# Clamp of the weight pieces on VectorE, bias tiles loaded one by one, and another order of the attention steps

## The chip, the cores and the metric

The kernel runs on one core of a Trainium2 chip. The metric is the time of one execution on the device in microseconds (us); runs of the same kernel are given by their median. The engines are TensorE (PE in the profile, its weight loads PEld), VectorE (DVE), ScalarE (ACT), GpSimd (POOL) and SyncE (SP), which issues most of the DMA transfers. Each engine works through its own queue in order and waits for others by semaphores.

## What is computed

Attention over 8 batches and 8 heads with a bias that depends on positions, and behind it two matrix products of a gated network on its output:

```python
scores = scale * np.matmul(q, k.transpose(0, 1, 3, 2))        # q, k, v: 8 x 8 x 576 x 64
x = (np.log1p(np.abs(rel)) / psi_i)[..., None]
bias = np.maximum(x @ w1 + b1, 0.0) @ w2                      # 576 x 576 x 8 heads
scores = scores + bias.transpose(2, 0, 1)[None]
attn = np.exp(scores - np.max(scores, axis=-1, keepdims=True))
attn = attn / (np.sum(attn, axis=-1, keepdims=True) + 1e-09)
x = np.matmul(attn, v)                                        # -> 4608 x 512
a, b = x @ moe_w1, x @ moe_w2                                 # 512 x 1024 each
h = a * b @ moe_w3                                            # 1024 x 1024
out = h @ moe_w_out                                           # 1024 x 512
```

The weights of the network arrive as 64-bit floating point and are made into 32-bit numbers on the chip, with integer and floating operations on their two halves.

## The kernel before

**Stages.** A prologue computes the bias for all heads and writes it to the DRAM tile `nb_d`. Then attention runs over 32 units, one for each pair of heads `p` (four) and batch `b` (eight), `u = 8p + b`. Then `w_out` is folded into `w3` (`fold`, 16 steps, and `evict_w`), while the first two weight matrices are made ready in 16 pieces (`split_w`). Last come nine chunks of 512 tokens, eight `up` and `down` steps each, which is dense work for PE.

**A unit of attention.** Its 576 rows for two heads are nine tiles, named 0 to 7 and M (even numbers are the first head, odd the second, M the last 64 rows of both). The steps are named by a letter and a tile:

- `ldk`, `ldq`, `ldv` load (SP); `gk`, `gq` (`op_g`, POOL) split k and q into a rounded part and a rest, `kh`, `kl`, `qh`, `ql`, in two buffers each.
- `S` (`op_S`, PE, L266): scores of a tile into one of two PSUM buffers, in three products.
- `T` (`op_T`, DVE, L277): adds the bias tile `nb`, scales, and finds the maximum. It frees the S buffer; its result is one of four buffers `ts`.
- `E` (`op_E`, ACT, L300): exponential and sum of the row.
- `F` (`op_F`, PE, L321 to L333): transposes. F0 to F3 take the two heads of a row block, FL the last 64 columns of all, FN what is left of M. `H` (`op_H`, L344 on DVE, L346 on ACT) copies each from PSUM to SBUF.
- `W0`, `W1` (`op_W`, PE, L386): product with v for columns 0 to 255 and 256 to 575. `X` (`op_X`) copies it out, `xd` stores it.
- In the last unit of a pair `r`, `R`, `HR`, `rd` make and store the reciprocal sums.
- `c0` to `c7` (in units 1 to 6 of each pair) make one 128 x 512 piece of `w_out` or `w3` into 32 bits by the eight steps of `narrow`: fetch (SP), size (ACT, L128), rest and clamp (POOL, L131 and L134), shift, head and power (DVE, L137, L143, L148), and total, two products on POOL (L151, L152). The raw piece `wi` has one buffer here, and two in the later 16 pieces.

Transposes and W share the PSUM pool `ps_t`, two buffers, taken in the order of PE: six F and one for both W0 and W1 in a unit. A step that takes a buffer waits for the copy that frees the one taken two before.

**What sets the order.** The table `ORDER` gives each step of a unit a time, and unit u is put `u * PERIOD` later; the times only sort the steps, engine by engine, for PE, DVE, ACT and POOL. So steps of up to four units stand interleaved in a queue. The loads' order on SP is chosen by the compiler. The later stages are sorted in the same way by `AT_F`, `PACE_F` (fold), `AT_W1`, `PACE_W` (weight pieces), `AT_X`, `PACE_X` (split of the first chunk's x).

**Bias tiles.** `load_bias` fetches the tiles of a pair in five groups, `02`, `13`, `46`, `57` and `M`, with one buffer each. A group of the next pair is loaded in the last unit of a pair, once both T's that read it are issued.

Of the kernel before, what the change touches and what calls it, by code (L numbers as in the profile page):

```python
# [9 lines left out]
F32 = mybir.dt.float32  # L10
F32R = mybir.dt.float32r
I32 = mybir.dt.int32
U32 = mybir.dt.uint32
AF = mybir.ActivationFunctionType
# [4 lines left out]
P = 128  # L19
# [6 lines left out]
AT_F, PACE_F = 2.50, 3.20  # L26
AT_FOLD = -2.0, -1.4, -1.3, -0.6, 0.0
AT_W1, PACE_W, AT_X, PACE_X = 4.00, 5.70, 37.00, 2.10
# [3 lines left out]
PERIOD = 13.21  # L32
ORDER = {
    "PE": {
        "S6": 0.00, "SM": 0.40, "S5": 1.75, "S7": 5.79, "S4": 6.19, "S3": 7.68, "S2": 9.48, "S1": 9.88, "S0": 15.85,
        "FN": 20.32, "F3": 20.46, "F1": 21.58, "FL": 22.43, "F2": 23.78, "F0": 28.20, "W0": 37.99, "W1": 43.25,
    },
    "DVE": {
        "T6": 0.60, "TM": 1.46, "T5": 4.84, "T7": 6.79, "T4": 7.94, "T3": 8.80, "T2": 10.96, "T1": 11.82, "c4": 16.12,
        "c5": 16.70, "c6": 17.40, "T0": 17.48, "HN": 21.15, "HL": 23.20, "H2": 26.18, "X": 46.49,  # L40
    },
    "ACT": {
        "E6": 2.03, "EM": 4.18, "E5": 5.73, "E7": 10.07, "E4": 11.05, "c1": 12.33, "E2": 12.59, "E3": 13.57,
        "E1": 14.55, "E0": 20.21, "H3": 21.23, "H1": 22.40, "H0": 30.01,
    },
    "POOL": {
        "gq": -7.23, "gk": -2.81, "c3": 13.11, "c2": 13.65, "c7": 17.80,
    },
    "SP": {"ldk": -13.62, "ldq": -15.83, "ldv": 7.34},
}  # L50
AT_R = 23.41
# [14 lines left out]
def relpos_attention_moe(  # L66
# [43 lines left out]
    def narrow(pool, src, n, x, queue, pieces=1):  # L110
# [19 lines left out]
        def rest():  # L130
            nc.gpsimd.tensor_scalar(x, d["lo"].bitcast(U32), 2.0 ** -52, 1.0, op0=ALU.mult, op1=ALU.mult)  # L131

        def clamp():
            nc.gpsimd.tensor_scalar(d["mag"], d["mag"], LEAST, MOST, op0=ALU.max, op1=ALU.min)  # L134
# [54 lines left out]
    nbp = att_r.enter_context(tc.tile_pool(name="nbp", bufs=1, side="right"))  # L189
# [16 lines left out]
    GROUPS = ("02", "13", "46", "57", "M")  # L206
    GROUP = {t: g for g in GROUPS for t in g}

    def load_bias(p, ts):
        if ts == "M":  # L210
            nb = nbp.tile([P, S], F32, name="nbM")
            nc.sync.dma_start(nb[lo], nb_v[2 * p, 512:576, :])
            nc.sync.dma_start(nb[hi, S - 512:S], nb_v[2 * p + 1, 512:576, 0:512])
            nc.sync.dma_start(nb[hi, 0:S - 512], nb_v[2 * p + 1, 512:576, 512:S])
            NB[p, ts] = nb
            return
        nb = nbp.tile([P, 2, S], F32, name=f"nb{ts[0]}")
        h, r0 = int(ts[0]) % 2, int(ts[0]) // 2 * P
        rows = nb_v[2 * p + h, r0:r0 + 2 * P, :].rearrange("(k p) j -> p k j", p=P)
        if h == 0:  # L220
            nc.sync.dma_start(nb, rows)
        else:
            nc.sync.dma_start(nb[:, :, S - 512:S], rows[:, :, 0:512])
            nc.sync.dma_start(nb[:, :, 0:S - 512], rows[:, :, 512:S])
        for k, t in enumerate(ts):
            NB[p, t] = nb[:, k]
# [44 lines left out]
    def op_T(u, t):  # L271

        d = st[u]
        p, b = units[u]
        ts = sm.tile([P, S], F32, name="ts", bufs=NTS)
        mx = sm.tile([P, 1], F32, name="mx", bufs=NTS)
        nc.vector.tensor_tensor_reduce(  # L277
            out=halves(ts), in0=d.pop(("s", t))[:, :, :HS], in1=halves(NB[p, t]),
            op0=ALU.add, op1=ALU.min, scale=-1.0 / SQ, scalar=3.0e38, accum_out=mx,
        )  # L280
        d["t", t] = (ts, mx)
        done = d.setdefault("done", set())
        done.add(t)
        if b == B - 1 and p + 1 < NPAIR and done.issuperset(GROUP[t]):
            load_bias(p + 1, GROUP[t])

# [54 lines left out]
    def move(on, *moves):  # L341
        for o, x in moves:
            if on == "DVE":
                nc.vector.tensor_copy(o, x)  # L344
            else:
                nc.scalar.activation(o, x, AF.Copy)  # L346
# [19 lines left out]
    def op_W(u, n):  # L366
# [4 lines left out]
        if "acc" not in d:  # L371
            d["acc"] = ps_t.tile([P, 2, 512], F32, name="pst")
        acc = d["acc"][:, int(n), 0:qs.stop - qs.start]
# [17 lines left out]
    def op_X(u, n, on):  # L391
        d = st[u]
        d["x"] = sm.tile([P, S], F32, name="x")
        move(on, *((d["x"][:, qs], d["acc"][:, m, 0:qs.stop - qs.start]) for m, qs in enumerate(QS)))
# [6 lines left out]
    def piece_of(i):  # L401
        if i < NF:
            return narrow(cva, moe_w_out[i * P:(i + 1) * P, :], DO, wos[i], nc.sync)
        hf, t = divmod(i - NF, NF)
        return narrow(cva, moe_w3[t * P:(t + 1) * P, hf * 512:(hf + 1) * 512], 512, w3s[t][hf], nc.sync)
# [25 lines left out]
    with ExitStack() as pro:  # L431
# [92 lines left out]
        for G in range(NGRP):  # L524
            at = -LEAD + G * PACE_B
            put(plan, bias_group(G), *(at + d for d in AT_BIAS))
            for ts in GROUPS:
                if G == (NGRP - 1 if ts == "M" else 8 * (int(ts[-1]) // 2) + 7):
                    plan.append((at + AT_BIAS[-1] + LAG_B, len(plan), lambda ts=ts: load_bias(0, ts)))
# [280 lines left out]
```

## Time and profile before

| | |
|---|---|
| three runs | 1258.41, 1259.74, 1261.9 us |
| median | 1259.74 us |
| profiled execution | 1257.73 us, span 1255.9 us, mean granted clock 0.971 |
| PE busy | 1132.2 us (90%) |
| DVE, ACT, POOL busy | 638.9, 521.4, 452.1 us |

The page divides the span into 40 equal slices of 31.4 us; each digit is the busy share of a slice in tenths, and PEclk is the granted clock of TensorE:

```profile
PE   8668878887888788889788999999999999999998
PEld 3246656665666666666466788888888888888887
DVE  8648766776677667767787522222212221313111
ACT  7557756676677667763232221212121212121211
POOL 0347754775477547747677400000000000000000
PEclk9879999999999999999988999999999999999999
```

The first two slices are the prologue, slices 3 to 17 attention, 18 to 22 the fold with the weight pieces, and the rest the `up` and `down` steps. A row of the trace's timeline reads: start, duration, engine, line, operation, output <- inputs, shapes, count, and in brackets how long the engine had been idle and what ended that. In the groups of instructions the bar is followed by total busy time, mean ns of one, and the idle time of the engine just ahead of them with what ended it.

### The profile page before, as it was taken

To read this page: it belongs to the slowest core of one execution; us is meant where nothing else is said; L and a number is where in the kernel's file an instruction comes from. 1 tells how busy PE (TensorE), PEld (TensorE's weight loads), DVE (VectorE), ACT (ScalarE), POOL (GpSimd) and SP (SyncE) were. 2 spreads that over 40 slices of the span, in tenths; PEclk is the share of its full clock that TensorE was granted. 3 is DMA by queue.
4 is the path that set the end of the run, shared out by engine and by line. 5 is a ranking of instruction groups with operands and counts; after the bars stand their busy time and mean duration, and the time that the engine had idled before them with its cause. 6 is when DMAs were issued, how large, how long until landed. Compare 5 with 4: busy or idle time off the path is not lost.

```text
span 1255.9 us, 22540 instructions
## 1 busy us (share of the span) xinstructions
PE 1132.2 (90%) x9092; PEld 881.3 (70%) x9092; DVE 638.9 (51%) x1288; ACT 521.4 (42%) x1039; POOL 452.1 (36%) x342
## 2 busy tenths in 40 slices
PE   8668878887888788889788999999999999999998
PEld 3246656665666666666466788888888888888887
DVE  8648766776677667767787522222212221313111
ACT  7557756676677667763232221212121212121211
POOL 0347754775477547747677400000000000000000
PEclk9879999999999999999988999999999999999999
DMA  7743453446344634431433111111111120200001
GB/s 220 246 151 115 139 198 122 135 136 201 122 136 136 201 121 136 135 101 45 137 125 100 51 67 34 57 45 51 51 51 51 36 65 34 68 34 1 23 12 33
DMA packets 61127, 123.13 MB, mean 98 GB/s; under 512 B 9312, under 2 KB 18912, under 8 KB 61024
## 3 DMA queue, kind: packets, MB, share of 16 engines
q1 hardware_dynamic: 59728, 120.21, 29.8%
q10 hardware_dynamic: 1296, 1.49, 0.4%
q8 instruction: 71, 1.16, 0.4%
q14 instruction: 32, 0.26, 0.1%
HBM read 91.76 MB, written 29.92 MB: 97 GB/s over the span
## 4 chain that ended last, share of the span: by engine, by line
PE 72%; DVE 7%; POOL 6%; DMA 6%; ACT 4%; issue 3%; SPq 1%; ACTq 0%; DVEq 0%; POOLq 0%
PE up L652 29%; PE o L677 15%; PE pst L386 12%; PE s L266 8%; PE pst L321 5%; DVE ts L277 4%; ACT pt L346 3%; DMA wi<-in_moe_w_dram 3%; PE bacc L504 2%; POOL wmag L134 2%; DVE x L344 2%; DMA nb_d<-bev 1%; DMA nb<-nb_d 1%; PE pst L332 1%; POOL w L151 1%
## 5 line engine op out<-in xcount | busy, mean ns | idle before, releaser
L277 DVE CUSTOM_DVE_ANT_0 ts<-s,nb 128x576 f32<-128x576 f32 x256 | 188.4, 753 | 131.5 <-PE s L266 95.9
L652 PE MATMUL up<-xh,wh 128*128 128x512 f32 x576 | 225.4, 391 | 0.0
L652 PE MATMUL up<-xh,wl 128*128 128x512 f32 x576 | 225.4, 391 | 0.0
L652 PE MATMUL up<-xl,wh 128*128 128x512 f32 x576 | 225.3, 391 | 0.0
L300 ACT ACTIVATE pp<-ts,mx 128x576 f32<-128x576 f32 x256 | 196.1, 769 | 69.4 <-DVE mx L277 69.4
L660 DVE TENSOR_TENSOR g<-up,a 128x512 f32<-128x512 f32 x72 | 49.7, 690 | 336.0 <-PE up L652 335.9
L677 PE MATMUL o<-w3s,gh 128*128 128x512 f32 x576 | 180.6, 395 | 3.7 <-ACT gh L663 3.7
L638 POOL TENSOR_SCALAR xh<-xr 128x512 fp32r<-128x512 f32 x36 | 23.8, 662 | 437.8 <-DVE xr L634 436.3
L386 PE MATMUL pst<-pt,rv 128*64 128x256 f32 (+1 forms) x1280 | 171.0, 413 | 0.5 <-DVE rt L344 0.5
L266 PE MATMUL s<-kh,qh 64*128 64x288 f32 x640 | 118.7, 363 | 34.5 <-DVE mx L277 31.9
L657 ACT COPY a<-up 128x512 f32<-128x512 f32 x72 | 42.1, 585 | 251.0 <-PE up L652 251.0
L321 PE MATMUL pst<-ident,pp 64*128 64x64 f32 x2304 | 108.3, 226 | 40.7 <-DVE x L344 39.8
L346 ACT ACTIVATE pt<-pst 128x1024 f32<-128x1024 f32 x96 | 96.2, 1025 | 95.1 <-PE pst L321 95.1
L321 PEld LDWEIGHTS pst<-ident,pp 64*128 64x128 f32 x2304 | 100.2, 141 | 47.9 <-issue 44.9
L386 PEld LDWEIGHTS pst<-pt,rv 128*64 128x64 f32 x1280 | 89.1, 139 | 63.3 <-issue 9.7
L677 PEld LDWEIGHTS o<-w3s,gh 128*128 128x128 f32 x576 | 109.5, 191 | 28.3 <-ACT gh L663 5.4
L652 PEld LDWEIGHTS up<-xh,wh 128*128 128x128 f32 x576 | 108.4, 188 | 23.4
L652 PEld LDWEIGHTS up<-xh,wl 128*128 128x128 f32 x576 | 108.4, 188 | 23.3
L652 PEld LDWEIGHTS up<-xl,wh 128*128 128x128 f32 x576 | 108.3, 188 | 23.4
L677 PE MATMUL o<-w3s,gl 128*128 128x512 f32 x288 | 114.5, 398 | 3.6 <-DVE gl L666 3.6
L663 ACT ACTIVATE gh<-g 128x512 fp32r<-128x512 f32 x72 | 45.5, 632 | 171.3 <-DVE g L660 171.3
L266 PEld LDWEIGHTS s<-kh,qh 64*128 64x128 f32 x640 | 64.6, 194 | 58.9 <-DVE mx L277 41.6
(86 smaller groups left out, 1794.6 us busy)
## 6 DMA issues: line engine op xcount, KB each, us to landing
rq<-in_q_dram SPq DMA_DIRECT2D x31, 640.0 KB
wi<-in_moe_w_dram SPq DMA_DIRECT2D x32, 512.0 KB
nb_d<-bev SPq DMA_DIRECT2D x36, 295.5 KB
rv<-in_v_dram SPq DMA_DIRECT2D x32, 320.0 KB
x_d<-x SPq DMA_DIRECT2D x32, 288.0 KB
xr<-x_d SPq DMA_DIRECT2D x36, 256.0 KB
rb<-r_d SPq DMA_DIRECT2D x72, 128.0 KB
rk<-in_k_dram SPq DMA_DIRECT2D x31, 288.0 KB
```

The costliest lines, as they stand in the source:

```text
L134: nc.gpsimd.tensor_scalar(d["mag"], d["mag"], LEAST, MOST, op0=ALU.max, op1=ALU.min)
L266: nc.tensor.matmul(s[:, hf, :HS], Q[x][rows, q0:q0 + P], K[y][rows, h * HS:(h + 1) * HS], start=(m == 0), stop=(m == len(ops) - 1),)
L277: nc.vector.tensor_tensor_reduce(out=halves(ts), in0=d.pop(("s", t))[:, :, :HS], in1=halves(NB[p, t]), op0=ALU.add, op1=ALU.min, scale=-1. ...
L300: nc.scalar.activation(pp, ts, AF.Exp, bias=mx, scale=-1.0, accum_out=sums[p][:, 9 * b + col:9 * b + col + 1])
L321: nc.tensor.transpose(ps[0:n, hf, c0:c0 + 64], x[rows], ident[rows, rows])
L346: nc.scalar.activation(o, x, AF.Copy)
L386: nc.tensor.matmul(o, x[:, c0:c0 + D], m, start=(c == 0), stop=(c == 4 and n_m == len(ms) - 1),)
L652: nc.tensor.matmul(acc, l[:, cc], r, start=(n == 0), stop=(n == 3 * NC - 1))
L657: nc.scalar.copy(a, ps[0])
L660: nc.vector.tensor_tensor(g, ps[1], a, op=ALU.mult)
L663: nc.scalar.activation(gh, g, AF.Copy)
L677: nc.tensor.matmul(d["o", t], l[:, sl], folded[ft][r], start=(ft == 0 and n == 0), stop=(ft == NF - 1 and n == 2),)
```

## The change

- **Clamp**: `clamp` of `narrow` is issued on VectorE, for all 40 pieces.
- **Rest**: for the 24 pieces made during attention `rest` stays on GpSimd; for the 16 later ones it is an activation on ScalarE.
- **Bias tiles**: nine tiles a pair, each loaded by itself into one of eleven buffers, in the order of their T's (`TURNS`). In the last unit but one of a pair the first two tiles of the next pair are loaded; in the last unit the T of each tile is followed by the load of the tile two further on. For the first pair each tile is loaded when its group of bias rows has been written.
- **W and X**: W0 and W1 take a PSUM buffer each, and X is two steps, X0 and X1.
- **Order**: new times for all steps, with a period of 12.49. E, F and H are distributed anew: H1, H0, HL and H2 on ACT, H3, HN, X0 and X1 on DVE; c3 (the clamp) on DVE.
- **Constants**: `AT_F`, `PACE_F` and `AT_X` are smaller.

```diff
@@ -23,32 +23,32 @@
 FIRST = {"ldk": -15.0, "ldq": -14.0, "ldv": -4.0, "gk": -9.0, "gq": -5.0}
 AT_BIAS = -0.7, 1.0, 2.5
 
-AT_F, PACE_F = 2.50, 3.20
+AT_F, PACE_F = 2.00, 2.80
 AT_FOLD = -2.0, -1.4, -1.3, -0.6, 0.0
-AT_W1, PACE_W, AT_X, PACE_X = 4.00, 5.70, 37.00, 2.10
+AT_W1, PACE_W, AT_X, PACE_X = 4.00, 5.70, 28.00, 2.10
 AT_W = 3.5, 0.0, 0.5, 1.2, 2.6, 3.8, 5.5, 7.1, 10.0, 10.6
 
 
-PERIOD = 13.21
+PERIOD = 12.49
 ORDER = {
     "PE": {
-        "S6": 0.00, "SM": 0.40, "S5": 1.75, "S7": 5.79, "S4": 6.19, "S3": 7.68, "S2": 9.48, "S1": 9.88, "S0": 15.85,
-        "FN": 20.32, "F3": 20.46, "F1": 21.58, "FL": 22.43, "F2": 23.78, "F0": 28.20, "W0": 37.99, "W1": 43.25,
+        "S0": 0.00, "S3": 0.41, "S1": 1.76, "S7": 2.29, "S5": 4.20, "S2": 7.21, "SM": 7.62, "S6": 9.04, "F1": 13.82,
+        "F0": 15.23, "S4": 15.85, "FL": 21.04, "F2": 25.88, "F3": 28.79, "W0": 29.67, "FN": 32.16, "W1": 34.51,
     },
     "DVE": {
-        "T6": 0.60, "TM": 1.46, "T5": 4.84, "T7": 6.79, "T4": 7.94, "T3": 8.80, "T2": 10.96, "T1": 11.82, "c4": 16.12,
-        "c5": 16.70, "c6": 17.40, "T0": 17.48, "HN": 21.15, "HL": 23.20, "H2": 26.18, "X": 46.49,
+        "T0": 0.71, "T3": 1.40, "T1": 2.43, "T7": 3.12, "T5": 6.30, "T2": 7.88, "c3": 9.03, "c4": 9.54, "TM": 10.13,
+        "T6": 10.82, "c5": 11.51, "c6": 12.36, "T4": 18.14, "H3": 29.51, "X0": 32.41, "HN": 33.63, "X1": 37.84,
     },
     "ACT": {
-        "E6": 2.03, "EM": 4.18, "E5": 5.73, "E7": 10.07, "E4": 11.05, "c1": 12.33, "E2": 12.59, "E3": 13.57,
-        "E1": 14.55, "E0": 20.21, "H3": 21.23, "H1": 22.40, "H0": 30.01,
+        "E0": 4.39, "E3": 5.18, "E1": 5.97, "c1": 7.61, "E5": 8.21, "E7": 9.29, "E2": 11.03, "E6": 11.82, "EM": 12.61,
+        "H1": 15.02, "H0": 15.97, "E4": 19.29, "HL": 22.61, "H2": 26.60,
     },
     "POOL": {
-        "gq": -7.23, "gk": -2.81, "c3": 13.11, "c2": 13.65, "c7": 17.80,
+        "gk": -8.54, "gq": -6.29, "c2": 10.54, "c7": 12.84,
     },
-    "SP": {"ldk": -13.62, "ldq": -15.83, "ldv": 7.34},
+    "SP": {"ldk": -18.63, "ldq": -14.18, "ldv": 0.74},
 }
-AT_R = 23.41
+AT_R = 22.64
 TILES = "01234567M"
 NPP, NTS, NPS = 7, 4, 2
 
@@ -107,7 +107,7 @@
     LEAST = struct.unpack("<f", struct.pack("<I", 0x38000000))[0]
     MOST = struct.unpack("<f", struct.pack("<I", 0x47EFFFFF))[0]
 
-    def narrow(pool, src, n, x, queue, pieces=1):
+    def narrow(pool, src, n, x, queue, pieces=1, low=nc.scalar):
 
         d = {}
 
@@ -128,10 +128,13 @@
             nc.scalar.activation(d["mag"], f(d["hi"]), AF.Abs)
 
         def rest():
-            nc.gpsimd.tensor_scalar(x, d["lo"].bitcast(U32), 2.0 ** -52, 1.0, op0=ALU.mult, op1=ALU.mult)
+            if low is nc.scalar:
+                nc.scalar.activation(x, d["lo"].bitcast(U32), AF.Copy, scale=2.0 ** -52)
+            else:
+                low.tensor_scalar(x, d["lo"].bitcast(U32), 2.0 ** -52, 1.0, op0=ALU.mult, op1=ALU.mult)
 
         def clamp():
-            nc.gpsimd.tensor_scalar(d["mag"], d["mag"], LEAST, MOST, op0=ALU.max, op1=ALU.min)
+            nc.vector.tensor_scalar(d["mag"], d["mag"], LEAST, MOST, op0=ALU.max, op1=ALU.min)
 
         def shift():
             nc.vector.tensor_scalar(
@@ -186,7 +189,7 @@
     att, att_r = ctx.enter_context(ExitStack()), ctx.enter_context(ExitStack())
     raw = att_r.enter_context(tc.tile_pool(name="raw", bufs=1, side="right"))
     qk = att_r.enter_context(tc.tile_pool(name="qk", bufs=1, side="right"))
-    nbp = att_r.enter_context(tc.tile_pool(name="nbp", bufs=1, side="right"))
+    nbp = att_r.enter_context(tc.tile_pool(name="nbp", bufs=11, side="right"))
     cva = att_r.enter_context(tc.tile_pool(name="cva", bufs=1, side="right"))
     ps_s = att_r.enter_context(tc.tile_pool(name="ps_s", bufs=2, space=PSUM, side="right"))
     vp = att.enter_context(tc.tile_pool(name="vp", bufs=2))
@@ -203,27 +206,24 @@
         return x.rearrange("p (a j) -> p a j", a=2)
 
 
-    GROUPS = ("02", "13", "46", "57", "M")
-    GROUP = {t: g for g in GROUPS for t in g}
-
-    def load_bias(p, ts):
-        if ts == "M":
-            nb = nbp.tile([P, S], F32, name="nbM")
-            nc.sync.dma_start(nb[lo], nb_v[2 * p, 512:576, :])
-            nc.sync.dma_start(nb[hi, S - 512:S], nb_v[2 * p + 1, 512:576, 0:512])
-            nc.sync.dma_start(nb[hi, 0:S - 512], nb_v[2 * p + 1, 512:576, 512:S])
-            NB[p, ts] = nb
-            return
-        nb = nbp.tile([P, 2, S], F32, name=f"nb{ts[0]}")
-        h, r0 = int(ts[0]) % 2, int(ts[0]) // 2 * P
-        rows = nb_v[2 * p + h, r0:r0 + 2 * P, :].rearrange("(k p) j -> p k j", p=P)
-        if h == 0:
-            nc.sync.dma_start(nb, rows)
-        else:
-            nc.sync.dma_start(nb[:, :, S - 512:S], rows[:, :, 0:512])
-            nc.sync.dma_start(nb[:, :, 0:S - 512], rows[:, :, 512:S])
-        for k, t in enumerate(ts):
-            NB[p, t] = nb[:, k]
+    TURNS = sorted(TILES, key=lambda t: ORDER["DVE"]["T" + t])
+
+    def load_bias(p, t, first=False):
+        nb = NB[p, t] if first else nbp.tile([P, S], F32, name="nb")
+        NB[p, t] = nb
+        heads = (0, 1) if t == "M" else (int(t) % 2,)
+        for h in heads:
+            o = nb[(lo, hi)[h]] if t == "M" else nb
+            r0 = 512 if t == "M" else int(t) // 2 * P
+            rows = nb_v[2 * p + h, r0:r0 + o.shape[0], :]
+            if h == 0:
+                nc.sync.dma_start(o, rows)
+            else:
+                nc.sync.dma_start(o[:, S - 512:S], rows[:, 0:512])
+                nc.sync.dma_start(o[:, 0:S - 512], rows[:, 512:S])
+
+    for t in TURNS:
+        NB[0, t] = nbp.tile([P, S], F32, name="nb")
 
     def load(u, which):
         p, b = units[u]
@@ -279,10 +279,12 @@
             op0=ALU.add, op1=ALU.min, scale=-1.0 / SQ, scalar=3.0e38, accum_out=mx,
         )
         d["t", t] = (ts, mx)
-        done = d.setdefault("done", set())
-        done.add(t)
-        if b == B - 1 and p + 1 < NPAIR and done.issuperset(GROUP[t]):
-            load_bias(p + 1, GROUP[t])
+        k = TURNS.index(t)
+        if p + 1 < NPAIR:
+            if b == B - 2 and k < 2:
+                load_bias(p + 1, t)
+            elif b == B - 1 and k + 2 < len(TURNS):
+                load_bias(p + 1, TURNS[k + 2])
 
     def op_E(u, t):
         d = st[u]
@@ -368,9 +370,7 @@
         d = st[u]
         qs, x = QS[int(n)], d["rv"]
         PT, PX = PTX[u % 2]
-        if "acc" not in d:
-            d["acc"] = ps_t.tile([P, 2, 512], F32, name="pst")
-        acc = d["acc"][:, int(n), 0:qs.stop - qs.start]
+        acc = ps_t.tile([P, 2, 512], F32, name="pst")[:, 0, 0:qs.stop - qs.start]
         for c in range(5):
             for h, rows in enumerate((lo, hi)):
                 c0 = (4 * h + c if c < 4 else 8 + h) * D
@@ -390,8 +390,9 @@
 
     def op_X(u, n, on):
         d = st[u]
-        d["x"] = sm.tile([P, S], F32, name="x")
-        move(on, *((d["x"][:, qs], d["acc"][:, m, 0:qs.stop - qs.start]) for m, qs in enumerate(QS)))
+        if "x" not in d:
+            d["x"] = sm.tile([P, S], F32, name="x")
+        move(on, (d["x"][:, QS[int(n)]], d["acc" + n]))
 
     def op_x(u, n):
         p, b = units[u]
@@ -400,9 +401,9 @@
 
     def piece_of(i):
         if i < NF:
-            return narrow(cva, moe_w_out[i * P:(i + 1) * P, :], DO, wos[i], nc.sync)
+            return narrow(cva, moe_w_out[i * P:(i + 1) * P, :], DO, wos[i], nc.sync, low=nc.gpsimd)
         hf, t = divmod(i - NF, NF)
-        return narrow(cva, moe_w3[t * P:(t + 1) * P, hf * 512:(hf + 1) * 512], 512, w3s[t][hf], nc.sync)
+        return narrow(cva, moe_w3[t * P:(t + 1) * P, hf * 512:(hf + 1) * 512], 512, w3s[t][hf], nc.sync, low=nc.gpsimd)
 
     pieces = dict(zip([u for u in range(NU) if 0 < u % B < B - 1], (piece_of(i) for i in range(3 * NF))))
     assert len(pieces) == 3 * NF
@@ -524,9 +525,9 @@
         for G in range(NGRP):
             at = -LEAD + G * PACE_B
             put(plan, bias_group(G), *(at + d for d in AT_BIAS))
-            for ts in GROUPS:
-                if G == (NGRP - 1 if ts == "M" else 8 * (int(ts[-1]) // 2) + 7):
-                    plan.append((at + AT_BIAS[-1] + LAG_B, len(plan), lambda ts=ts: load_bias(0, ts)))
+            for t in TILES:
+                if G == (NGRP - 1 if t == "M" else 8 * (int(t) // 2) + 7):
+                    plan.append((at + AT_BIAS[-1] + LAG_B, len(plan), lambda t=t: load_bias(0, t, True)))
         drive(plan)
 
 
```

## The prediction

> **What bounds the kernel now.** I read busy time by stage first, then one unit of attention instruction by instruction, then the step from one pair of heads to the next, then the chain of waits after attention.
>
> ```profile
> 105.28:542.46 437.18, 375.22 (x5215) 289.85 (x5213) 314.12 (x748) 294.89 (x613) 289.28 (x202) 0.97 0.46 147
> ...
> 567.61:715.30 147.69, 123.70 (x545) 91.40 (x544) 109.14 (x123) 42.82 (x74) 104.35 (x78) 0.92 0.31 97
> 715.30:1255.90 540.60, 536.32 (x2352) 441.60 (x2351) 127.88 (x190) 96.80 (x166) 17.31 (x28) 1.00 0.13 41
> ```
> The columns are length, then busy time of PE, PEld, DVE, ACT, POOL, then granted clock, DMA share, GB/s. The last stage (the second part of the network, 540.6 us) is PE at 99%: the change does not touch it. What can move lies ahead: units 3 to 31 of attention start between 105.28 and 542.46 (28 intervals, PE idle 62 us), and the fold stage, where the weight pieces are made (PE idle 24 us, clock 0.92).
>
> Inside a unit, VectorE and TensorE:
> ```profile
> 253.51 0.34 PE L386 MATMUL pst<-px,rv 128*64 128x64 f32 x4
> ...
> 256.23 0.72 PE L321 MATMUL pst<-ident,pp 64*128 64x64 f32 x16 [1.34 <-DVE x L344]
> ```
> ```profile
> 254.59 0.76 DVE L277 CUSTOM_DVE_ANT_0 ts<-s,nb 128x576 f32<-128x576 f32 x1 [1.57 <-PE s L266]
> ...
> 255.27 0.82 DVE L344 COPY x<-pst 128x256 f32<-128x256 f32 x2
> ...
> 269.99 0.82 DVE L344 COPY x<-pst 128x256 f32<-128x256 f32 x2
> ```
> A unit takes 269.99 - 255.27 = 14.72 us. W1 has ended at 253.85, but its eviction X stands behind a T that waits for an S issued after W1; DVE idles 1.57 us, X starts at 255.27, and PE waits 1.34 us for the PSUM buffer. Two such units together, groups with idle time:
> ```profile
> L266 PE MATMUL s<-kh,qh 64*128 64x288 f32 x40 | 7.2, 350 | 0.4 <-DVE mx L277 0.4
> L321 PE MATMUL pst<-ident,pp 64*128 64x64 f32 x144 | 6.7, 223 | 2.7 <-DVE x L344 2.7
> L332 PE MATMUL pst<-ident,ppM 64*128 64x64 f32 x8 | 1.3, 235 | 0.3 <-ACT pt L346 0.3
> ```
> PE idles 3.4 us in two units, so its own work is 14.72 - 1.7 = 13.0 us a unit.
>
> Between pairs of heads:
> ```profile
> 172.33 0.82 DVE L344 COPY x<-pst 128x256 f32<-128x256 f32 x2
> ...
> 178.02 0.38 SPq L221 DMA_DIRECT2D nb<-nb_d  x1
> ...
> 185.09 0.76 DVE L277 CUSTOM_DVE_ANT_0 ts<-s,nb 128x576 f32<-128x576 f32 x1 [5.50 <-DMA nb<-nb_d]
> ...
> 194.12 0.82 DVE L344 COPY x<-pst 128x256 f32<-128x256 f32 x2
> ```
> The tile of two bias blocks is loaded only after the last T that reads it, 7 us ahead of its next use; that unit takes 21.79 us, 7.07 more than 14.72. There are three such places. Check: 28 x 14.72 + 3 x 7.07 = 433.4 of the 437.2 us.
>
> After attention, one cycle of a weight piece in the chain of waits:
> ```profile
> 643.09 0.79 POOL w L131
> ...
> 643.95 1.97 POOL wmag L134
> 645.92 1.27 POOL w L151
> ...
> 647.22 3.61 DMA wi<-in_moe_w_dram
> ...
> 650.91 0.70 ACT wmag L128
> ...
> 654.96 3.64 DMA wi<-in_moe_w_dram
> ```
> ```profile
> 567.61 0.65 POOL L131 TENSOR_SCALAR w<-wi 128x512 f32<-128x512 uint32 x1
> ...
> 700.03 0.64 POOL L131 TENSOR_SCALAR w<-wi 128x512 f32<-128x512 uint32 x1 [1.79 <-DMA wi<-in_moe_w_dram]
> ```
> Load, rest, clamp, then the previous piece's product frees the buffer for the next load: 654.96 - 647.22 = 7.74 us each, all on POOL and DMA. The 16 pieces take 132.4 us for 15 intervals, 8.8 each with the fold among them.
>
> **The change, part by part.**
>
> (1) The order. Folded into one period, the new list has PE run S0 S3 F2 F1 S1 S7 F0 S4 F3 S5 W0 FN S2 SM FL S6 W1, where F2, F3, W0, FN, W1 belong to two units back and F1, F0, S4, FL to one back. I walk it with the waits of these rows:
> ```profile
> 262.41 0.40 PE L266 MATMUL s<-kh,qh 64*128 64x288 f32 x2
> ...
> 264.04 0.40 PE L266 MATMUL s<-kh,qh 64*128 64x288 f32 x2 [0.18 <-DVE mx L277]
> ```
> ```profile
> 263.22 0.76 DVE L277 CUSTOM_DVE_ANT_0 ts<-s,nb 128x576 f32<-128x576 f32 x1 [0.69 <-PE s L266]
> ...
> 264.02 0.76 DVE L277 CUSTOM_DVE_ANT_0 ts<-s,nbM 128x576 f32<-128x576 f32 x1
> 264.70 0.42 DVE L137 TENSOR_SCALAR wmag<-wmag 128x512 int32<-128x512 int32 x1
> 265.16 0.69 DVE L143 SCALAR_TENSOR_TENSOR wmag<-wi,wmag 128x512 int32<-128x512 int32 x1
> 265.96 0.43 DVE L148 TENSOR_SCALAR wi<-wmag 128x512 int32<-128x512 int32 x1
> ```
> ```profile
> L300 ACT ACTIVATE pp<-ts,mx 128x576 f32<-128x576 f32 x256 | 196.1, 769 | 69.4 <-DVE mx L277 69.4
> ```
> T may start 0.81 after its S (262.41 to 263.22), occupies DVE 0.68 (264.02 to 264.70), and frees the S buffer 0.82 after its start (264.04); an eviction frees its PSUM buffer 0.14 after its end (X above: 256.09 to 256.23). With S at 0.4 to 0.5 start to start, F at 0.5, W0 at 2.3 and W1 at 2.9 (rounded from that same unit), PE goes, from S0 = 0: S3 0.5, F2 0.9, F1 1.4, S1 1.9, S7 2.35, F0 2.8, S4 3.5 (held 0.2 for T1, which waits for S1), F3 4.0, S5 4.5, W0 5.0, FN 7.3, S2 7.5, SM 8.0, FL 8.8, S6 9.3, W1 9.85, next S0 12.75. That is PE's own work again, as the 13.0 above says. Of its releases: X1 now stands ahead of T0 and needs no later S, so it runs as W1 ends (0.2 to 0.8) and F1 at 1.4 finds it done; F0 follows H2 (done 2.7), W0 follows H0 (4.6), FL follows X0 (8.1). W0 and W1 have a PSUM allocation each, eight a period on two buffers where seven stood, and each finds the eviction two back finished. So the 1.34 goes and nothing of its size takes its place; late next would be F0 behind H2, by 0.1 or so. I take **12.9** for a unit without a weight piece.
>
> (2) The clamp in attention. DVE gains one instruction a piece (c3), which I price at 0.42 like L137 above, its nearest row in shape and engine (the other end is POOL's own, 1.97 in the chain of waits). Where it is put is dearer. c3 follows HN, 5.5 to 6 us after S4, and POOL, which starts the next unit's split when S4 frees the k buffer, is then in ql, after kh, kl and qh (the rows show them in the old order):
> ```profile
> 254.36 1.26 POOL L249 TENSOR_SCALAR qh<-rq 128x1280 fp32r<-128x1280 f32 x1
> 255.70 2.92 POOL L250 TENSOR_TENSOR ql<-rq,qh 128x1280 fp32r<-128x1280 f32 x1
> ...
> 259.34 1.42 POOL L250 TENSOR_TENSOR kl<-rk,kh 128x576 fp32r<-128x576 f32 x1
> ```
> ```profile
> 661.45 1.29 POOL L151 TENSOR_TENSOR w<-w,wi 128x512 f32<-128x512 f32 x1
> ```
> ```profile
> 661.51 1.51 DVE L137 TENSOR_SCALAR wmag<-wmag 128x512 int32<-128x512 int32 x1 [1.81 <-POOL wmag L134]
> ```
> The same L137 takes 0.42 beside an idle POOL and 1.51 beside a POOL tensor_tensor, ending 0.28 after it (663.02 against 662.74). So c3 cannot end before ql. The whole split takes 260.76 - 254.36 = 6.40. The chain: S4 + 0.75 (its four steps of PE and the hand-over), split 6.40, +0.28 = S4 + 7.4; c4 0.45 to 0.9, TM and T6 1.36, c5 0.8 (265.16 to 265.96), c6 0.43 give X1 at S4 + 10.4 to 10.9; from X1 over T0, S1, T1 to the next S4 it is 0.40 + 3 x 0.82 = 2.86. Together 13.2 to 13.7; I take **13.5**. [...]
> What is late is X1 again, behind c3 to c6, and F1 behind it. 22 of the 28 units carry a piece: (22 x 13.5 + 6 x 12.9) / 28 = 13.37, a gain of 28 x 1.35 = **38 us**. [...]
>
> (3) Bias tiles singly, eleven buffers. Two tiles of the next pair load a unit early, each other one two T's after its predecessor, so more than 13 us ahead of use against 7 before. Six more DMA issues a pair cost SP about 0.4 each, which nothing waits for. The whole 7.07 should go; I take **20 us** of 21 for three (bounds 0, 21).
>
> (4) The start.
> ```profile
> 69.37 0.76 DVE L277 CUSTOM_DVE_ANT_0 ts<-s,nb 128x576 f32<-128x576 f32 x1 [18.88 <-DMA nb<-nb_d]
> ...
> 74.67 0.76 DVE L277 CUSTOM_DVE_ANT_0 ts<-s,nbM 128x576 f32<-128x576 f32 x1 [4.53 <-DMA nbM<-nb_d]
> ```
> T6 and TM lead unit 0 now, and both wait for late bias; the other seven T's come behind them. In the new order six T's stand ahead of TM, three of them on the early blocks: by 75 us seven are done instead of two. Five T's by 0.8 to 1.2 us (S, T and the S buffer take turns, 0.81 + 0.82 over two buffers) are 4 to 6; with the next unit's first S's close behind I take **6 us** (bounds 0, and 9 for all seven).
>
> (5) The last 16 pieces. Rest goes to ACT (busy 42.8 of 147.7, so 0.65 hides beside the clamp's wait), the clamp to DVE: POOL loses 0.79 + 1.97 a piece. A buffer's chain is then load 3.64, abs 0.70, clamp 0.42, shift 0.42, head 0.69, power 0.43, product 1.29, with six hand-overs some 8.5 us over two buffers, 4.3 a piece; but DVE's instructions with SBUF operands (those four, and wl like head: 2.65) and POOL's two products (2.6) take turns, and three differences of g and x, like head too, come to each second piece (1.0): 6.3, with hand-overs **6.7** where 7.74 stood. In the fold half 0.79 + 1.97 - 0.42 = 2.3 a piece could go, but its steps, the load of x and POOL's differences of the fold also wait: half of it. 8 x 1.0 + 8 x 1.2 is about **17 us** (bounds 0 and 34: PE's idle 24 plus the 8% of clock on 124). AT_F, PACE_F and AT_X only reorder inside this stage.
>
> Sum: 38 + 20 + 6 + 17 = 81. The profiled execution took 1257.73 (span 1255.9); 1257.7 - 81 = 1176.7. The median shown, 1259.74, is 2 us above it: **1179 us**.
>
> **Rivals.**
> [...]
> B, the gains outside the unit fail: the tail stays at POOL's and DMA's pace because loads, x and the fold wait in turn, or the bias loads still collide: 17 to 30 us worse, 1196 to 1209. That is the clamp not doing what it says, too.
> C, the slower side: the piece's load comes late.
> ```profile
> SPq L237 <- POOL ql L250: 119.8, 27, 12.6
> ```
> ```profile
> 253.06 0.33 SPq L123 DMA_DIRECT2D wi<-in_moe_w_dram  x1
> ```
> SP serves loads in a fixed row and idles 119.8 us in the queue ahead of q loads that wait for ql. c1 on ACT now stands ahead of E5, E7 and the rest, 4 us after S4 (T4 behind H3 2.4, E4 0.8 later and 0.8 long). The piece's one buffer comes free with the product behind c6, about 1.4 before the next S4, and the load lands some 3.8 later: a slack of 1.6. If wi comes behind the q load instead, it lands 11 us after S4: ACT and then PE lose about 6 us in 22 units, 132 us: 1179 + 132 = 1311. It decides from 1.6 + 81/22 = 5.3 us of lateness. Against it: wi is issued now at 253.06, just as its buffer comes free.
>
> **How the numbers follow.** The forecast itself has 0.52 (1167 to 1192), A 0.15, B 0.20, something smaller lost in several places 0.07 (1210 to 1250), C 0.06. The range, 1150 to 1218, leaves out C, most of the 0.07 and the far ends of A and B. Changes under 0.3%, 4 us, cannot be told from none: faster 0.92, same 0.02, slower 0.06.
>
> **What would show it.** X spaced 13.3 to 13.7 with pieces and about 12.9 without; no PE idle put down to DVE x of 1.34; c3 as a max/min on DVE of over 1 us ending 0.3 after ql; no wait of T for nb over 2 us between pairs; TM of unit 0 near 74 with six T's ahead; pieces 6.5 to 8 apart, and the last up stage again 540 us long. Long ACT idle ahead of L128 would show C, and would make me wrong.

## The result, and the profile after

The changed kernel takes 1173.92 us (median of four runs, 1170.18 to 1179.22) against 1259.08 us for the kernel before (1253.79 to 1261.9): a ratio of 0.9331, with a 95% interval of 0.9281 to 0.9382. The forecast was 1179. The profiled execution took 1171.91 us with a span of 1170.1, 85.8 less than the 1257.73 of before.

The 40 slices of the page, of 29.3 us each now:

```profile
PE   7669998998999999999999999999999999999998
DVE  8748878888888788849985322213131322213111
POOL 0446665775567467525453000000000000000000
PEclk9889999999999999999999999999999999999999
```

From slice 4 on PE no longer falls to 7, and the dense part begins at slice 22 of shorter slices.

By stage, in the same columns as before (length, busy time of PE, PEld, DVE, ACT, POOL, then granted clock, DMA share, GB/s). The stages are: up to the first S of unit 3, up to that of unit 31, most of unit 31, the fold, and the last part. The last part begins here with the same up step as before; that step starts at 629.14, where it started at 715.13.

```profile
0.00:103.80 103.80, 74.70 (x708) 41.04 (x710) 73.50 (x191) 70.35 (x157) 34.72 (x30) 0.90 0.67 206
103.80:488.65 384.85, 366.69 (x5213) 286.06 (x5213) 328.82 (x742) 313.69 (x639) 248.63 (x178) 1.00 0.53 164
488.65:515.00 26.35, 24.41 (x318) 17.72 (x317) 14.51 (x35) 21.47 (x41) 6.74 (x5) 1.00 0.23 76
515.00:629.14 114.14, 109.30 (x510) 83.87 (x507) 101.17 (x138) 48.39 (x84) 57.42 (x44) 0.99 0.40 126
629.14:1170.10 540.96, 536.82 (x2353) 441.39 (x2351) 129.16 (x192) 97.95 (x168) 18.98 (x30) 1.00 0.13 41
```

The 28 units went from 437.18 to 384.85 us (52.3 less), the start from 105.28 to 103.80 (1.5 less), and everything behind the start of unit 31 from 1255.9 - 542.46 = 713.4 to 681.4 (32 less). The last part is as long as it was (541 us), so these 32 us lie ahead of it: the fold takes 114.1 us instead of 147.5. PE is busy 96% of that time at a clock of 0.99, where it was 84% at 0.92.

One unit with a weight piece in the changed kernel, VectorE and GpSimd together (timeline):

```profile
261.70 0.42 DVE L346 COPY x<-pst 128x256 f32<-128x256 f32 x1 [0.19 <-PE pst L386]
261.85 2.95 POOL L250 TENSOR_TENSOR ql<-rq,qh 128x1280 fp32r<-128x1280 f32 x1
262.47 0.76 DVE L277 CUSTOM_DVE_ANT_0 ts<-s,nb 128x576 f32<-128x576 f32 x1 [0.34 <-PE s L266]
...
263.64 1.45 DVE L137 TENSOR_SCALAR wmag<-wmag 128x512 f32<-128x512 f32 x1
...
268.47 0.48 DVE L346 COPY x<-pst 128x320 f32<-128x320 f32 x1
...
275.27 0.42 DVE L346 COPY x<-pst 128x256 f32<-128x256 f32 x1 [0.19 <-PE pst L386]
...
287.90 0.42 DVE L346 COPY x<-pst 128x256 f32<-128x256 f32 x1 [0.19 <-PE pst L386]
```

X0 comes every 275.27 - 261.70 = 13.57 us with a piece and 287.90 - 275.27 = 12.63 without. c3 (L137 is the clamp here) starts while ql runs and takes 1.45; ql ends at 264.80, c3 at 265.09. The T in front of it, whose operand comes from PSUM, keeps its 0.76 beside the same ql.

Behind a pair of heads, the same view with PE:

```profile
288.06 2.93 POOL L250 TENSOR_TENSOR ql<-rq,qh 128x1280 fp32r<-128x1280 f32 x1
...
288.24 2.80 DVE L307 TENSOR_SCALAR sum<-sum 128x72 f32<-128x72 f32 x1
...
292.36 0.40 PE L266 MATMUL s<-kh,qh 64*128 64x288 f32 x2 [2.55 <-DVE mx L277]
...
292.95 2.86 PE L386 MATMUL pst<-pt,rv 128*64 128x320 f32 x20
```

```profile
303.55 0.42 DVE L346 COPY x<-pst 128x256 f32<-128x256 f32 x1 [0.18 <-PE pst L386]
```

T no longer waits for bias tiles there. But the unit takes 303.55 - 287.90 = 15.65 us: r, a tiny instruction (72 columns), takes 2.80 us beside ql, T's stand behind it, and PE idles 2.55.

### The profile page after: what moved, and what is told of

Its sections match the earlier page's. It is cut to its first block, busy times and chain, and to the rows that moved or that the text cites. A ratio compares the mean times of both kernels' runs of the same rounds, so it can differ in the third digit from the quotient of the medians.

```text
span 1170.1 us, 22602 instructions
## 1 busy us (share of the span) xinstructions
PE 1111.9 (95%) x9092; PEld 870.1 (74%) x9092; DVE 647.2 (55%) x1296; ACT 551.9 (47%) x1087; POOL 366.5 (31%) x286
## 4 chain that ended last, share of the span: by engine, by line
PE 51%; DVE 5%; ACT 3%; DMA 3%; POOL 1%; issue 1%; ACTq 0%; SPq 0%; DVEq 0%; POOLq 0%
PE up L653 30%; PE o L678 15%; DMA wi<-in_moe_w_dram 3%; PE pst L386 2%; PE s L266 2%; DVE wmag L137 1%; DVE ts L277 1%; PE pst L323 1%; POOL w L154 1%; PE wacc L611 1%; ACT pp L302 1%; DVE w3l L604 1%; ACT wmag L128 0%; DVE wmag L140 0%; ACT ppM L302 0%
## 5 line engine op out<-in xcount | busy, mean ns | idle before, releaser
L277 DVE CUSTOM_DVE_ANT_0 ts<-s,nb 128x576 f32<-128x576 f32 x288 | 207.5, 753 | 41.8 <-PE s L266 27.2
L678 PE MATMUL o<-w3s,gh 128*128 128x512 f32 x576 | 177.8, 390 | 0.3 <-ACT gh L664 0.3
L348 ACT ACTIVATE pt<-pst 128x1024 f32<-128x1024 f32 x128 | 126.3, 1013 | 34.5 <-PE pst L323 34.5
L386 PEld LDWEIGHTS pst<-pt,rv 128*64 128x64 f32 x1280 | 88.1, 137 | 62.4 <-issue 11.5
L323 PE MATMUL pst<-ident,pp 64*128 64x64 f32 x2304 | 104.9, 224 | 11.1 <-ACT ppM L302 10.7
L266 PE MATMUL s<-kh,ql 64*128 64x288 f32 x640 | 96.6, 295 | 2.4 <-POOL ql L250 2.4
```

Of the source, the lines that this page charges most:

```text
L266: nc.tensor.matmul(s[:, hf, :HS], Q[x][rows, q0:q0 + P], K[y][rows, h * HS:(h + 1) * HS], start=(m == 0), stop=(m == len(ops) - 1),)
L277: nc.vector.tensor_tensor_reduce(out=halves(ts), in0=d.pop(("s", t))[:, :, :HS], in1=halves(NB[p, t]), op0=ALU.add, op1=ALU.min, scale=-1. ...
L323: nc.tensor.transpose(ps[0:n, hf, c0:c0 + 64], x[rows], ident[rows, rows])
L386: nc.tensor.matmul(o, x[:, c0:c0 + D], m, start=(c == 0), stop=(c == 4 and n_m == len(ms) - 1),)
L678: nc.tensor.matmul(d["o", t], l[:, sl], folded[ft][r], start=(ft == 0 and n == 0), stop=(ft == NF - 1 and n == 2),)
```

## The experiments

All times are medians; each edit is made on the changed kernel (1173.92 us) unless said otherwise. X0 spacings are read as above.

### The clamp later on VectorE

```diff
-"c3": 9.03, "c4": 9.54, "TM": 10.13,
+"c3": 11.40, "c4": 11.45, "TM": 10.13,
```

> The changed kernel with c3 and c4 put behind T6 on VectorE, so that TM and T6 no longer stand behind a clamp that waits for ql. If the clamp's wait beside ql is what makes units with a weight piece longer than those without (13.58 against 12.63 us in the trace), these units fall to 12.6 to 12.9: 22 units by 0.7 to 0.9, some 15 to 20 us off 1174, about 1156. If they are longer only because VectorE has four more instructions a piece, the period stays at 13.4 to 13.6 and the time within 4 us of 1174. If X1, which follows c6, comes later for it, units grow and the time is above 1180.

Measured: 1153.18 us (1150.34 to 1154.71), ratio 0.9171 (0.9135 to 0.9208). Timeline of VectorE and GpSimd, one unit:

```profile
240.60 0.43 DVE L346 COPY x<-pst 128x256 f32<-128x256 f32 x1 [0.19 <-PE pst L386]
240.75 2.95 POOL L250 TENSOR_TENSOR ql<-rq,qh 128x1280 fp32r<-128x1280 f32 x1
...
242.53 0.76 DVE L277 CUSTOM_DVE_ANT_0 ts<-s,nb 128x576 f32<-128x576 f32 x1
243.22 0.75 DVE L277 CUSTOM_DVE_ANT_0 ts<-s,nb 128x576 f32<-128x576 f32 x1
243.78 0.70 POOL L134 TENSOR_SCALAR w3s<-wi 128x512 f32<-128x512 uint32 x1
243.89 0.88 DVE L137 TENSOR_SCALAR wmag<-wmag 128x512 f32<-128x512 f32 x1
...
253.25 0.42 DVE L346 COPY x<-pst 128x256 f32<-128x256 f32 x1 [0.18 <-PE pst L386]
```

And a stretch of about four units in the windows view:

```profile
207.00:257.00 50.00, 49.99 (x744) 39.77 (x742) 43.87 (x108) 44.69 (x91) 38.10 (x28) 1.00 0.54 169
```

Units take 12.65 us with a piece and without: the two T's run while ql does, the clamp comes behind it, and PE is busy 49.99 of 50 us. VectorE still executes the four instructions. So it was the wait that cost 0.92 a unit, not the work. The units behind a pair got longer here, 17.3 us each.

### The reciprocal sums later

```diff
-AT_R = 22.64
+AT_R = 23.60
...
-at.update(r=(max(at["E" + t][0] for t in TILES) + 1.0, "DVE"), ...
+at.update(r=(max(at["E" + t][0] for t in TILES) + 4.2, "DVE"), ...
```

> The changed kernel with step r of each pair (and R, HR, rd with it) moved behind T6 of the next unit. If the 15.6 us of the unit behind a pair come from r, which takes 2.80 us on VectorE beside ql, that unit falls to about 12.7 to 13.2 and the time by 3 x 2.5 = 7 to 9 us, to about 1166. If the loads of the bias tiles or the transposition R hold that unit, it stays at 15 us or more and the time within 4 us of 1174.

Measured: 1162.41 us (1160.89 to 1163.02), ratio 0.9245 (0.9211 to 0.9280). Timeline of VectorE:

```profile
287.97 0.19 DVE L307 TENSOR_SCALAR sum<-sum 128x72 f32<-128x72 f32 x1
```

r takes 0.19 again, the three units behind a pair take 12.87 to 12.89, and 11.5 us are gone, more than expected, because those units had been dearer than 15.6 in some places (17.28 once in the trace of the changed kernel). The spread of the runs falls from 9 us to 2. What may lie behind both is in the section on hardware below.

### The clamp of the attention pieces back on GpSimd

```diff
-"c3": 9.03, "c4": 9.54, "TM": 10.13,
+"c4": 11.45, "TM": 10.13,
...
-"gk": -8.54, "gq": -6.29, "c2": 10.54, "c7": 12.84,
+"gk": -8.54, "gq": -6.29, "c3": 10.50, "c2": 10.54, "c7": 12.84,
...
-nc.vector.tensor_scalar(d["mag"], d["mag"], LEAST, MOST, op0=ALU.max, op1=ALU.min)
+(nc.vector if low is nc.scalar else nc.gpsimd).tensor_scalar(d["mag"], d["mag"], LEAST, MOST, op0=ALU.max, op1=ALU.min)
```

> The changed kernel with the clamp of the 24 attention pieces back on GpSimd (c3 there ahead of c2, c4 on VectorE behind T6); the later 16 pieces stay as changed. If the new order alone made the units shorter and the place of the clamp adds or takes only the wait beside ql, units with a piece take 12.8 to 13.3 and the time falls 5 to 17 us below 1174. If the clamp had to leave GpSimd for the new order to hold, because c4, c6 and X1 now wait for GpSimd's clamp behind ql and its 1.97 us, units take 14 us or more and the time is above 1184.

Measured: 1182.88 us (1181.48 to 1185.08), ratio 0.9416 (0.9373 to 0.9459). Timeline:

```profile
268.23 1.91 POOL L137 TENSOR_SCALAR wmag<-wmag 128x512 f32<-128x512 f32 x1
...
270.18 0.43 DVE L140 TENSOR_SCALAR wmag<-wmag 128x512 int32<-128x512 int32 x1 [1.76 <-POOL wmag L137]
...
272.11 0.48 DVE L346 COPY x<-pst 128x320 f32<-128x320 f32 x1
...
272.74 0.72 PE L323 MATMUL pst<-ident,pp 64*128 64x64 f32 x16 [0.93 <-DVE x L346]
```

Units with a piece take 13.87: between the two expectations, nearer to the second, and slower than the change's 13.57. GpSimd's clamp can only start when ql has ended (268.14) and takes 1.91; VectorE waits 1.76 for it, and X1 with PE (0.93) behind it. Placed as in the change, the clamp on VectorE gains 0.3 us a unit over this; placed behind T6, 1.2. That is 22 x 0.3 = 6.6 of the 9 us lost; the rest fits the units behind a pair, 17.2 to 17.3 in this trace.

### The kernel before with X ahead of T7

```diff
-"X": 46.49,
+"X": 46.40,
```

> The kernel before with one time changed: X goes ahead of T7 on VectorE instead of behind it, and nothing else. If the 14.72 us of its units come from X waiting behind a T whose scores are issued after W1, the unit falls by 1.3 us to about 13.4 and the time by 28 x 1.3 = 36 us, to about 1222. If another chain (GpSimd's split and clamp) stands close behind, the unit falls by 0.3 us or less and the time stays above 1249.

Measured: 1205.94 us (1200.39 to 1208.96) against 1257.98, ratio 0.9588 (0.9544 to 0.9632). Timeline of VectorE:

```profile
250.84 0.82 DVE L344 COPY x<-pst 128x256 f32<-128x256 f32 x2 [0.77 <-PE pst L386]
...
264.17 0.82 DVE L344 COPY x<-pst 128x256 f32<-128x256 f32 x2 [0.66 <-PE pst L386]
```

```profile
174.61 0.76 DVE L277 CUSTOM_DVE_ANT_0 ts<-s,nb 128x576 f32<-128x576 f32 x1 [1.58 <-DMA nb<-nb_d]
```

The unit falls to 13.33, as the reading of X behind T said, and the gain is 52 us, not 36. Most of the rest lies between pairs: the two units that the step touches take 31.0 to 31.4 us together, where they took 36.8 to 37.4, and T waits 1.58 for the bias tile instead of 5.50 (2.29 and 2.94 instead of 5.67 and 4.35 at the later two), with the loads still in groups. From the first X to the 29th, one exchange of neighbours in the old order brings 48.4 us by the traces, where the whole change brings 51.7.

### The bias tiles in five groups again

```diff
-nbp = att_r.enter_context(tc.tile_pool(name="nbp", bufs=11, side="right"))
+nbp = att_r.enter_context(tc.tile_pool(name="nbp", bufs=1, side="right"))
+GROUPS = ("02", "13", "46", "57", "M")
...
+if b == B - 1 and p + 1 < NPAIR and done.issuperset(GROUP[t]):
+    load_bias(p + 1, GROUP[t])
```

> The changed kernel with the bias tiles loaded in the five old groups, one buffer each, and all else as changed. If single tiles are what took the 7.07 us of each step between pairs away, this run loses 3 x 5 to 7 us plus some at the start, to 1189 to 1196. If the new order of the T's (first tile of a pair used 5.3 us after the last T of its group instead of at once) already hides most of the load, or the wait of r beside ql covers it, it loses under 6 us, at most 1180.

Measured: 1193.01 us (1188.57 to 1197.28), ratio 0.9492 (0.9461 to 0.9524). Timeline of VectorE at the first pair's end:

```profile
175.77 0.76 DVE L280 CUSTOM_DVE_ANT_0 ts<-s,nb 128x576 f32<-128x576 f32 x1 [4.42 <-DMA nb<-nb_d]
```

The wait is back, on top of r's: the two units that a step touches take 33.3 to 35.1 us together, against 28.2 to 29.9 in the changed kernel. Single tiles are worth 17 to 19 us here, and nothing at the start.

### The last 16 pieces

Three kernels take back parts of what changed there: clamp and rest on GpSimd (the first diff), the clamp alone (its last two lines), and the old times (the second diff).

```diff
-if low is nc.scalar:
+if False:
...
-    low.tensor_scalar(x, d["lo"].bitcast(U32), 2.0 ** -52, 1.0, op0=ALU.mult, op1=ALU.mult)
+    nc.gpsimd.tensor_scalar(x, d["lo"].bitcast(U32), 2.0 ** -52, 1.0, op0=ALU.mult, op1=ALU.mult)
...
-nc.vector.tensor_scalar(d["mag"], d["mag"], LEAST, MOST, op0=ALU.max, op1=ALU.min)
+(nc.gpsimd if low is nc.scalar else nc.vector).tensor_scalar(d["mag"], d["mag"], LEAST, MOST, op0=ALU.max, op1=ALU.min)
```

> The changed kernel with clamp and rest of the last 16 pieces both back on GpSimd; attention as changed. From the start of the last unit to the end the change gained 32 us where 17 were forecast. If the two moved steps carry it, this run gives back 25 to 32 us, to about 1202, and the pieces go from 7.0 us each to 8.5 or more. If the smaller times of the fold and of x's split carry about half, it gives back 10 to 17 us, to about 1187.

> The changed kernel with only the clamp of the last 16 pieces back on GpSimd, rest on ScalarE as changed. If GpSimd's own work a piece (1.97 for the clamp against 0.79 for the rest) sets the pace, most of what both steps together give comes back, 16 x 1.3 = 20 us, to about 1194. If the shared wait of VectorE beside GpSimd's products sets it, the clamp on VectorE brought little there, and the time stays below 1180.

```diff
-AT_F, PACE_F = 2.00, 2.80
+AT_F, PACE_F = 2.50, 3.20
-AT_W1, PACE_W, AT_X, PACE_X = 4.00, 5.70, 28.00, 2.10
+AT_W1, PACE_W, AT_X, PACE_X = 4.00, 5.70, 37.00, 2.10
```

> The changed kernel with the three old times of the fold and of the split of the first chunk's x (2.50, 3.20 and 37.00). If these times carry a part of the 32 us after attention, the run loses 8 to 15 us, to 1182 to 1189. If they only sort what waits for the weight pieces anyway, as the prediction had it, it stays within 4 us of 1174.

Measured: both steps back 1198.02 (0.9530, interval 0.9503 to 0.9557), the clamp alone 1195.18 (0.9510, 0.9479 to 0.9542), the old times 1188.71 (0.9435, 0.9386 to 0.9484). By these medians the clamp accounts for most of the 24 us of both steps, and the times for up to 15. But attention isn't touched by these edits, and yet in the traces of the last two kernels it took 6 us longer, all of it in the units behind a pair (17.28, 18.56 and 18.63 us with the old times, against 15.61, 15.65 and 17.28). From the third last X0 on, where those units are past, the three traces lose 22.8, 17.9 and 10.3 us. To have the sizes without that in whole runs, two of them were repeated on a kernel in which those units are mended.

### Both moves together, and the repeats

The clamp and r both behind T6:

> The changed kernel with both moves together: c3 and c4 behind T6, and r (with R, HR, rd) behind T6 of the unit after a pair. If the two waits beside ql are separate, units take 12.65 us throughout, those behind a pair too (17.3 with c3 moved alone), and the time falls by 3 x 4.6 = 14 us below 1153, to about 1139. If c3's move already took up the slack that r's move uses, the unit behind a pair stays at 14 us or more and the time above 1146.

Measured: **1139.2 us** (1138.19 to 1140.62), ratio 0.9067 (0.9049 to 0.9084). The two waits are separate: 12.65 in every unit, 12.88 behind a pair. That is 35 us below the changed kernel, and no other version is clearly faster. On it, first the old times, then clamp and rest of the last 16 pieces on GpSimd:

> The kernel with both moves (c3, c4 and r behind T6), which has no slow unit behind a pair, and the three old times of the fold and of x's split. If the 15 us that these times cost on the changed kernel were the fold's, about 10 by its trace, with 5 to 6 from the units behind a pair, this run is 8 to 12 us above 1139. If all of it was chance in the units behind a pair, it is within 4 us of 1139.

> The kernel with both moves and clamp and rest of the last 16 pieces back on GpSimd. On the changed kernel this cost 24 us, 23 of them after the last but two units by its trace. If that is the size of the step, this run is 20 to 25 us above 1139, at 1159 to 1164. If part of it was chance in the units behind a pair, it is under 17 us above.

Measured: 1149.19 (0.9165, 0.9144 to 0.9186), so the times are worth 10 us; 1162.55 (0.9269, 0.9248 to 0.9291), so the two steps are worth 23. (By the ratios to the kernel before, which was run beside each, it is 12 and 25.) Timeline of GpSimd in the second, and its first and last product:

```profile
572.08 0.80 POOL L134 TENSOR_SCALAR w<-wi 128x512 f32<-128x512 uint32 x1 [2.40 <-DMA wi<-in_moe_w_dram]
572.96 2.24 POOL L137 TENSOR_SCALAR wmag<-wmag 128x512 f32<-128x512 f32 x1
575.17 1.29 POOL L154 TENSOR_TENSOR w<-w,wi 128x512 f32<-128x512 f32 x1
```

```profile
493.00 1.29 POOL L154 TENSOR_TENSOR w<-w,wi 128x512 f32<-128x512 f32 x1
...
620.48 1.29 POOL L154 TENSOR_TENSOR w<-w,wi 128x512 f32<-128x512 f32 x1 [2.17 <-DVE wi L151]
```

The same two products in the version with both moves, clamp and rest as changed:

```profile
490.41 1.27 POOL L154 TENSOR_TENSOR w<-w,wi 128x512 f32<-128x512 f32 x1
...
595.58 1.29 POOL L154 TENSOR_TENSOR w<-w,wi 128x512 f32<-128x512 f32 x1 [2.23 <-issue]
```

15 intervals take 127.5 us (8.5 each) with rest and clamp in GpSimd's queue behind the load, and 105.2 (7.0) without: 22.3 of the 23 us. The old times do something else: their pieces take 108.8, and 6.3 us more lie behind the last product (548.1 against 541.8), because PE has less of the fold and the first up steps done by then: in the 125 us from 482 it executes 500 matmuls instead of 562. The kernel before had 547.8 there.

### The first unit in the order of its bias rows

In the changed kernel, as in the version with both moves, the fourth T waits for a late bias tile (timeline of VectorE, changed kernel):

```profile
72.21 0.76 DVE L277 CUSTOM_DVE_ANT_0 ts<-s,nb 128x576 f32<-128x576 f32 x1 [7.82 <-DMA nb<-nb_d]
```

On the version with both moves, in unit 0 alone, S7 and T7 go behind T2, SM and TM behind the next unit's T3:

```diff
-FIRST = {"ldk": -15.0, "ldq": -14.0, "ldv": -4.0, "gk": -9.0, "gq": -5.0}
+FIRST = {"ldk": -15.0, "ldq": -14.0, "ldv": -4.0, "gk": -9.0, "gq": -5.0, "S7": 8.0, "T7": 8.6, "E7": 11.3, "SM": 13.5, "TM": 14.5, "EM": 17.0}
```

> As the run with both moves, and in the first unit alone S7 and T7 stand behind T2 and SM and TM behind the second unit's T3, so that the tiles whose bias rows are written last come last. If the start fell short of its forecast because T7 and TM wait for their bias tiles with other T's behind them, this gives 3 to 5 us over that run, about 1135. If the start waits for the bias rows themselves and the first weight piece, it gives nothing, within 4 us of it.

Measured: 1138.15 us (1137.37 to 1140.95), ratio 0.9062 (0.9044 to 0.9081): no difference from 1139.2. Two windows of its trace:

```profile
70.00:80.00 10.00, 6.83 (x74) 6.48 (x74) 4.46 (x12) 4.03 (x10) 0.00 (x0) 0.66 0.69 217
80.00:90.00 10.00, 7.19 (x94) 5.83 (x90) 6.38 (x16) 9.58 (x22) 6.89 (x5) 0.83 0.31 97
```

Two more T's are done by 72 us (five instead of three), but by the 17th T the lead is gone (87.27 us, against 86.71). In the first of these windows PE's granted clock is 0.66, in the second 0.83, with ACT busy 9.58 of 10. The version with both moves has nearly the same there (0.66 and 0.75, and 9.44 of 10), so either may be what takes the lead away; the runs don't tell them apart.

## Why the prediction was right, and where it was not

- **The order, units (part 1 and 2).** Forecast 12.9 without and 13.5 with a piece, 38 us. Measured 12.63 and 13.57: 28 x 14.72 - (22 x 13.57 + 6 x 12.63) = 37.8. That the sum is met so closely is partly luck: units with a piece are 0.07 longer than forecast and those without 0.27 shorter, 1.5 us against 1.6. PE's own work, taken as 13.0, is 12.65 (busy 49.99 of 50 us with c3 moved). Both halves of the reasoning were shown: X behind a T held the old unit (X moved alone: 13.33), and c3 ends only behind ql (forecast 0.28 after it, measured 0.29). Rival A, no wait beside ql, is what the moved clamp brings about, at 12.65; the change itself didn't.
- **Bias tiles (part 3).** Forecast 20 of 21 us. What is over in the stretch of 28 units fell from 437.2 - 412.2 = 25.0 to 384.85 - 374.3 = 10.5: 14.5 gained. The step that failed is "the whole 7.07 should go": the wait for the tiles went, but r, which the new order puts beside ql, took 2.6 us more than alone, and the unit behind a pair lost 3 to 4.6: those three units are all of the 10.5. What was read for c3, that it ends only behind ql, held for r just as well (2.80 us, ending 0.05 behind it); the prediction looked only at the step that changed engines and not at the others that the new order set beside ql. And part of the 7.07 had been the order's, as the exchange of X and T7 shows.
- **The start (part 4).** Forecast 6, measured 1.5. The T's do come earlier (the first at 60.25 instead of 69.37, and six by 75 us, where the forecast had seven and the kernel before two). The step that failed is that five T's ahead are worth 4 to 6 us: the run with another order in the first unit shows that more T's ahead bring nothing. What eats the lead, PE's low clock or ACT's backlog, stays open.
- **The last 16 pieces (part 5).** Forecast 17, measured 32. Counted by the first product of each piece, the first seven intervals took 9.31 us each before and 8.06 after: 1.25 less, as forecast (1.2). The last eight took 7.78 and take 6.07: 1.7 less, where the forecast had 1.0. So the pace of 6.7 was mis-sized: it let VectorE's instructions and GpSimd's products take turns in every piece. The rows of the prediction show that for L137 alone (1.51 against 0.42); in the changed kernel's 16 pieces the clamp was held in nine (1.3 to 1.5 us) and the shift in eleven (0.83 to 1.41), but head in three (0.98 to 1.19), wl in two (1.09 and 1.28) and power in one (0.83). Together the pieces gave 22.4 us, and taking clamp and rest back costs 22.3 in them. And the step "AT_F, PACE_F and AT_X only reorder inside this stage" failed: these times are worth about 10, 6 of them behind the last product.
- **The sum.** 38 + 20 + 6 + 17 = 81 stands against 37.8 + 14.5 + 1.5 + 32 = 85.8. The total is close by luck: the shortfall of 10 and the excess of 15 partly cancel. Only for the unit were the waits and their sizes right.
- **Rivals.** B, the gains outside the unit fail, came in part at two places and was outweighed at the third. C, the late piece, did not come: the load is still issued as its buffer comes free, right behind the product (268.64 + 1.28).

```profile
269.94 0.33 SPq L123 DMA_DIRECT2D wi<-in_moe_w_dram  x1
```

## What to carry to other kernels

Before placing an instruction on VectorE whose operands all lie in SBUF, look at what GpSimd runs at that time: here the clamp and r, started while ql ran, took 1.45 and 2.80 us instead of 0.42 and 0.19, ended only 0.29 and 0.05 behind it, and everything behind them in the queue waited. Put such instructions behind those that read PSUM: with the clamp and r behind T6, units took 12.65 us, and 12.88 behind a pair. After a reordering, walk all steps along the busy stretches of the other engine, not only those that the change names.

## What the runs showed of the hardware

**An instruction's size says little beside ql.** The clamp, 512 columns, takes 0.42 us alone and 1.45 beside ql; r, 72 columns, 0.19 alone and 2.80. What counted was how long ql still ran: the clamp ends 0.29 after it, r 0.05. Beside a GpSimd tensor_scalar it is the same: with c3 behind T6 the clamp takes 0.88 and ends 0.29 after the rest of 0.70 (244.77 against 244.48). In these rows r and the clamp, whose operands all lie in SBUF, are held; T, whose scores lie in PSUM, takes 0.70 to 0.76 at all 288 places in the changed kernel, and the copy of X0 from PSUM 0.42 on average over all 32, beside ql too (262.47 and 261.70 above). A clamp that starts ahead of GpSimd's instruction is not held either: 0.42 at 579.46, with a product from 579.68. What makes the one wait for the other, the runs do not show.

**Behind a gap of 2.5 us on PE the granted clock was 1.00, 0.68 or 0.53.** In the kernel with the old times, the same r beside the same ql, timeline of PE, and the windows view around it:

```profile
294.19 0.60 PE L266 MATMUL s<-kh,qh 64*128 64x288 f32 x2 [2.53 <-DVE mx L277]
...
295.20 5.39 PE L386 MATMUL pst<-pt,rv 128*64 128x320 f32 x20
```

```profile
294.10:300.80 6.70, 6.62 (x31) 3.56 (x31) 1.92 (x8) 2.49 (x6) 0.00 (x0) 0.53 0.24 87
```

The same W1 took 2.86 us in the changed kernel after a gap of 2.55, at a clock of 1.00, and takes 5.39 here after 2.53, at a granted clock of 0.53. The changed kernel's own third gap lies between; the clock over the 5.3 us from there is 0.68:

```profile
401.95 0.40 PE L266 MATMUL s<-kh,qh 64*128 64x288 f32 x2 [2.52 <-DVE mx L277]
...
402.55 4.50 PE L386 MATMUL pst<-pt,rv 128*64 128x320 f32 x20
```

So the price of the gap is 3.0, 4.6 or 6.0 us, and that is where the units of 15.6, 17.3 and 18.6 us come from. The attention code is the same in both kernels, and the changed kernel's three gaps are as long as each other (2.53, 2.55 and 2.52 us, with a clock of 1.00, 1.00 and 0.68 over the next 5.3), so it looks like chance; what decides it no run here shows. It may account for most of the 9 us between runs of the changed kernel: the versions with r in place spread by 3.6 to 11.4 us over their runs, those with r moved by 2.0 to 3.6.
